# Two Q products moved behind the first half of the attention, and the gate/up pieces of the second half re-ordered

## The chip, the cores and the metric

One Trainium2 chip, one core of it. The metric is the device time of one execution in microseconds (us). The kernel before takes 743.94 us (median of 3 runs, 742.64 to 744.77). The sets of rounds ran on different chips, so each kernel is compared with the kernel before in its own rounds.

## The reference, cut to what matters

```python
x = A_x                                     # 1 x 2048 x 1024, bfloat16
def _A_ref(x, wqkv, wo):                    # linear attention, 32 heads of 32
    q, k, v = ...                           # x @ wqkv
    pq, pk = phi(q), phi(k)                 # phi(t) = where(t > 0, t + 1, exp(t)) + 1e-6
    kv = einsum("bhsd,bhse->bhde", pk, v);  z = einsum("bhsd->bhd", pk)
    o = (pq . kv) / (pq . z + 1e-6)
    return o.reshape(B, S, D) @ wo
def _B_ref(x, W_gate, W_up, W_down):        # inner size 3584
    return (relu(x @ W_gate) * (x @ W_up)) @ W_down
h  = x + _A_ref(_layernorm(x), A_wqkv, A_wo)
h2 = h + _B_ref(_layernorm(h), B_W_gate, B_W_up, B_W_down)
```

All tokens go through kv and z first; then each token needs Q, the denominators and numerators ("nd"), the output projection with wo, a layer norm, and the gate/up and down products.

## The kernel before

It computes the large products with a Strassen-like scheme of seven block products instead of eight. `strassen` is a generator: each `yield` ends a "piece" (mostly eight matmuls of 128x512), and the caller chooses what stands between two pieces. `A`, `E`, `D` are PSUM banks, `snap` is a copy of a bank by ScalarE, `fin` ends one quarter of the result.

```python
def strassen(pool, work, mm, fin, sbufs=3):
    ...
    for v in range(2):
        A[v] = pool.tile(...); mm(A[v], 1, v, True); snap(v, "m1")
    yield
    m2(0)
    for v in range(2):
        mm(A[v], 6, v, False); snap(v, "u2")
    m2(1)
    yield
    for v in range(2):
        E[v] = pool.tile(...); mm(E[v], 5, v, True)
    yield
    for v in range(2):
        mm(A[v], 7, v, False); snap(v, "u3"); fin(1, 1, v, E[v], snaps["u3", v])
    yield
    for v in range(2):
        mm(A[v], 4, v, False); fin(1, 0, v, A[v], None)
    yield
    for v in range(2):
        mm(E[v], 3, v, False); fin(0, 1, v, E[v], snaps["u2", v])
    yield
```

The attention works on 16 tiles of 128 tokens, in steps. In step n the five stages below run for tiles n, n-1, n-1, n-2 and n-4 (`LAG`):

```python
def nd():        # 8 matmuls of 128x132 in 3 banks "ab"; ScalarE Ln and Exp give 1/den (rd);
                 # VectorE writes o_sb = nd * rd (2 buffers)
def oT():        # DMA transpose of o_sb
def x_in():      # loads x_res (3 buffers)
def wo_h(borrow):# "attn": 2 x 8 matmuls in a bank "ab", or "E" when borrowed (steps 8 to 11);
                 # VectorE adds the residual into x_res; ScalarE normalizes into hn (2 buffers)
def hn_T():      # DMA transpose of hn into hnT; then the left sums hs for gate/up (VectorE)
```

Two Q units (of six pieces) for the second half's tokens are spread over the first eight steps as filler, the first gate/up units ("quads", of six pieces) over the later ones. The first piece of a quad, `begin`, also makes eight weight sums on VectorE.

```python
rest = [p for s in range(1, NS) for c in range(0, KH, 2) for p in [q_unit(s, c)] * 6]   # 12 pieces
for step in range(QSTEPS):                                                             # 8 steps
    now = rest[step * len(rest) // QSTEPS:(step + 1) * len(rest) // QSTEPS]
    ...
    attn_step(step)
    if step:                # eight loads of gate/up weights, 512 KB each
        for _ in range(-(-len(early_loads) // (QSTEPS - step))):
            early_loads.pop(0)(held[step][0:1, 0:1])
    for p in now:
        next(p)
...
for step in range(QSTEPS, ready):            # steps 8 to 11
    if step == QSTEPS:
        flow.pop(0)()                        # begin of the first quad
    attn_step(step)
for n in range(steps):                       # steps 12 to 19, 23 pieces
    attn_step(ready + n)
    for p in flow[n * len(flow) // steps:(n + 1) * len(flow) // steps]:
        p()
```

A scheduler then orders each engine's instructions; the order on TensorE is not just that of the program. In the profiles the Q products are line 438 (454 after the change), nd 511 (527), attn 541 (557), the first quads' products 705 (726), the main gate/up stage 785 (810).

## Time and profile before

| stretch | us | PE busy | what runs |
|---|---|---|---|
| 0 to 150 | 150 | | K, V, Q of the first half |
| 150 to 195 | 45 | 43.6 | attention, first half; Q pieces as filler |
| 195 to 222 | 27 | 23.4 | steps 8 to 11, almost no filler |
| 222 to 291 | 69 | 66.9 | attention, second half; gate/up pieces as filler |
| 291 to 737 | 446 | 444.3 | gate/up and down, TensorE without gaps |

The page of the kernel before: busy us and share of the span of each engine, then the granted TensorE clock in 40 slices.

```profile
PE 721.8 (97%) x3967; PEld 382.0 (52%) x4020; DVE 563.2 (76%) x991; ACT 322.0 (43%) x580; POOL 5.7 (1%) x44
PEclk9999999999999999999999999999999999999999
```

There are 4020 weight loads but 3967 matmuls: 53 matmul records are missing from this trace. They show as holes of one matmul without a releaser and are no idle time.

The windows view of the kernel before (start:end, length, busy us of PE, PEld, DVE, ACT and POOL with their counts, granted clock, DMA share, GB/s), for the three stretches that the change touches:

```profile
150.00:195.00 45.00, 43.60 (x238) 21.14 (x241) 31.13 (x74) 34.36 (x87) 1.58 (x7) 1.00 0.94 199
195.00:222.00 27.00, 23.40 (x132) 11.52 (x134) 24.32 (x71) 21.68 (x70) 0.31 (x1) 1.00 0.84 194
222.00:291.00 69.00, 66.92 (x320) 30.65 (x324) 50.39 (x124) 41.16 (x94) 0.00 (x0) 1.00 0.56 146
```

The waits of TensorE in the kernel before, 150 to 291 us: who waited, for whom, us in total, times, longest.

```profile
PE Eq L705 <- DVE hs L117: 2.0, 1, 2.0
PE Aq L438 <- ACT u L154: 1.1, 1, 1.1
PE nd L511 <- DVE o_sb L518: 1.0, 2, 0.8
PE Aq L705 <- ACT m L154: 0.7, 1, 0.7
PE Aq L705 <- ACT u L154: 0.6, 2, 0.3
PE attn L541 <- DVE o_sb L518: 0.4, 1, 0.4
PE attn L541 <- DMA oT<-o_sb: 0.3, 1, 0.3
```

The first two lines are what the change aims at. The timeline of TensorE in the kernel before shows both places (start, length, instruction, count, idle time before it and its releaser):

```profile
186.28 1.46 PE L438 MATMUL Aq<-xT,tq 128*128 128x512 bf16 x5 [1.10 <-ACT u L154]
...
216.79 0.51 PE L511 MATMUL nd<-kvz,pq_mem 128*128 128x132 bf16 x6
218.06 0.28 PE L511 MATMUL nd<-kvz,pq_mem 128*128 128x132 bf16 x2 [0.76 <-DVE o_sb L518]
220.34 0.59 PE L705 MATMUL Eq<-hs,tg 128*128 128x512 f16 x2 [2.00 <-DVE hs L117]
```

What ends the second wait stands in the chain of waits of the kernel before, 204 to 224 us (start, length, what):

```profile
212.57 1.24 ACT hn L557
...
215.62 4.21 DMA hn<-hn
...
219.85 0.44 DVE hs L117
...
220.34 0.59 PE Eq L705 x2
```

The last normalized tile of the first half is made, transposed by DMA, summed on VectorE, and only then can gate/up product 5 start.

**How lost time is counted here.** The timeline merges matmuls, and the modelled length of one (379 ns) is longer than the distance of two starts (216 ns), so short gaps hide in it. All sums of lost time below add, over single matmuls, the start-to-start distance beyond N/2.4 GHz + 2.5 ns, where that is over 60 ns, without one-matmul holes. That cadence is what the Trainium skill gives in "TensorE: Matmul & The Clock Gate", section "Wait — 56ns, not 53.3ns?"; traces agree (eight matmuls in 1.73 us).

### The profile page before, as it was taken

Reading aid. Unit: us, or ns where it says so; the run is one execution under the profiler, and the core shown is the slowest. Engines: PE = TensorE matmul, PEld = TensorE weight load, DVE = VectorE, ACT = ScalarE, POOL = GpSimd, SP = SyncE. Lnnn points to the kernel's source line nnn. Section 1 sums busy time; section 2 is a strip of 40 time slices with the busy share of each in tenths; the row PEclk is TensorE's granted clock in tenths of the full one; section 3 lists DMA queues with packets and bytes.
Section 4 is the critical chain, followed back from the end, with each engine's and each line's share of the span. In section 5 each row is a group of like instructions: output and inputs, shape, how many; then the busy total and the mean of one; then the engine's idle time right before and its main releaser. Section 6 shows DMA issues by size and latency. Waiting matters only on the chain.

```text
span 740.6 us, 10570 instructions
## 1 busy us (share of the span) xinstructions
PE 721.8 (97%) x3967; PEld 382.0 (52%) x4020; DVE 563.2 (76%) x991; ACT 322.0 (43%) x580; POOL 5.7 (1%) x44
## 2 busy tenths in 40 slices
PE   7999999999989999999999999999999999999997
PEld 3444555444444444444444444444444458888666
DVE  6997653675887767778778777877787479996797
ACT  4786553778686654444344434443435120000000
POOL 0000000000000000000000000000000000000000
PEclk9999999999999999999999999999999999999999
DMA  9765003079797526164638359475483399988822
GB/s 319 167 140 157 0 1 107 9 155 242 152 223 165 138 73 203 46 181 137 196 127 233 109 181 288 162 221 201 170 271 127 124 396 345 326 286 298 300 79 79
DMA packets 146579, 132.03 MB, mean 178 GB/s; under 512 B 50912, under 2 KB 128096, under 8 KB 146528
## 3 DMA queue, kind: packets, MB, share of 16 engines
q1 hardware_dynamic: 135392, 123.23, 55.3%
q10 hardware_dynamic: 11136, 8.13, 3.4%
q8 instruction: 31, 0.51, 0.3%
q14 instruction: 20, 0.16, 0.1%
HBM read 79.95 MB, written 39.85 MB: 162 GB/s over the span
## 4 chain that ended last, share of the span: by engine, by line
PE 78%; DVE 8%; ACT 7%; DMA 5%; issue 2%; SPq 0%; DVEq 0%; POOL 0%; ACTq 0%
PE accA L785 22%; PE accX L785 8%; PE accY L785 8%; PE accA L1117 8%; PE Aq L298 3%; PE accA L946 3%; PE accX L1117 3%; PE Aq L438 3%; DMA hn<-hn 2%; PE accY L1117 2%; PE attn L541 2%; PE Aq L705 2%; PE Eq L298 2%; PE accY L946 2%; PE accX L946 2%
## 5 line engine op out<-in xcount | busy, mean ns | idle before, releaser
L795 ACT ACTIVATE gu<-gu 128x512 bf16<-128x512 bf16 x72 | 45.4, 631 | 131.5 <-DVE gu L794 131.5
L790 ACT COPY snap<-accA 128x1024 f32<-128x1024 f32 x72 | 72.5, 1008 | 36.3 <-PE accA L785 36.2
L785 PEld LDWEIGHTS <-tg 128*128 128x128 f16 x384 | 37.6, 98 | 45.3
L785 PEld LDWEIGHTS <-tu 128*128 128x128 f16 x384 | 37.6, 98 | 45.3
L541 PE MATMUL attn<-wo_mem,oT 128*128 128x512 bf16 x249 | 57.9, 379 | 1.2 <-DVE o_sb L518 0.4
L794 DVE TENSOR_TENSOR gu<-accY,snap 128x1024 bf16<-128x1024 f32 x36 | 43.9, 1219 | 10.0 <-ACT snap L790 10.0
L785 PE MATMUL accA<-hn,tu 128*128 128x512 f16 (+1 forms) x192 | 49.3, 379 | 0.0
L785 PE MATMUL accA<-hn,tg 128*128 128x512 f16 (+1 forms) x192 | 49.3, 379 | 0.0
L794 DVE TENSOR_TENSOR gu<-accX,snap 128x1024 bf16<-128x1024 f32 x36 | 43.9, 1219 | 6.2 <-PE accX L785 3.7
L154 ACT COPY u<-Aq 128x512 f32<-128x512 f32 x56 | 32.4, 582 | 37.3 <-PE Aq L298 19.3
L1117 PEld LDWEIGHTS <-x 128*128 128x128 f16 (+1 forms) x448 | 43.8, 98 | 5.5
L785 PEld LDWEIGHTS <-wg 128*128 128x128 bf16 x288 | 28.2, 98 | 34.0
L785 PEld LDWEIGHTS <-wu 128*128 128x128 bf16 x288 | 28.2, 98 | 34.0
L541 PEld LDWEIGHTS <-oT 128*128 128x128 bf16 x256 | 24.6, 98 | 30.8 <-issue 2.9
L798 DVE TENSOR_TENSOR hq<-gu 128x512 bf16<-128x512 bf16 x48 | 20.3, 423 | 14.3 <-ACT gu L795 14.2
L298 PEld LDWEIGHTS <-xT 128*128 128x128 bf16 (+1 forms) x192 | 18.6, 98 | 23.7 <-issue 2.3
L1117 PEld LDWEIGHTS <-xs 128*128 128x128 f16 x280 | 27.4, 98 | 3.2
L543 DVE SCALAR_TENSOR_TENSOR x_res<-attn,x_res 128x512 bf16<-128x512 f32 x32 | 21.8, 687 | 7.2 <-PE attn L541 7.1
L946 PEld LDWEIGHTS <-x 128*128 128x128 bf16 (+1 forms) x168 | 16.4, 98 | 19.6
L518 DVE TENSOR_TENSOR o_sb<-nd,rd 128x384 bf16<-128x384 f32 (+1 forms) x48 | 22.8, 507 | 4.5 <-ACT rd L517 4.4
L1123 DVE TENSOR_TENSOR snap<-accA,u 128x1024 f32<-128x1024 f32 x16 | 19.5, 1220 | 8.3 <-PE accA L1117 8.0
L785 PE MATMUL accA<-hn,wu 128*128 128x512 bf16 x96 | 24.6, 379 | 0.0
(232 smaller groups left out, 1400.8 us busy)
## 6 DMA issues: line engine op xcount, KB each, us to landing
x<-x_dram SPq DMA_DIRECT2D x17, 896.0 KB, 8.2
x_dram<-hq SPq DMA_DIRECT2D x28, 512.0 KB, 3.1
wg<-in_B_W_gate_dram SPq DMA_DIRECT2D x14, 512.0 KB, 5.2
wu<-in_B_W_up_dram SPq DMA_DIRECT2D x14, 512.0 KB, 7.3
wraw<-in_B_W_down_dram SPq DMA_DIRECT2D x14, 512.0 KB, 4.8
x_dram<-hq SPq DMA_DIRECT2D x28, 256.0 KB, 2.6
t_dram<-wt SPq DMA_DIRECT2D x28, 256.0 KB, 2.2
xd<-x_dram SPq DMA_DIRECT2D x6, 896.0 KB, 7.1
```

The lines of the kernel that those rows point to most:

```text
L154: nc.scalar.copy(out=snaps[nm, v], in_=A[v][:])
L298: nc.tensor.matmul(ps[:], lhsT=left[m - 1][:, kc, r + v * P:r + (v + 1) * P], rhs=right[m - 1][:, kc, :], start=(start and kc == 0), stop= ...
L438: nc.tensor.matmul(ps[:], lhsT=rq[m - 1][:, kc, (c + v) * P:(c + v + 1) * P], rhs=left[m - 1][:, kc, :], start=(start and kc == 0), stop=( ...
L518: nc.vector.tensor_tensor(out=ov[:, c0:c0 + n], in0=ndv[:, :, 0:P].rearrange("p k (h e) -> p k h e", h=HPC), in1=rd[:, 0:n, :].unsqueeze(3 ...
L541: nc.tensor.matmul(ps[:], lhsT=st["oT"][:, c, :], rhs=wo_sb[:, c, j * NW:(j + 1) * NW], start=(c == 0), stop=(c == KC - 1))
L543: nc.vector.scalar_tensor_tensor(out=h_sb[:, j * NW:(j + 1) * NW], in0=ps[:], scalar=1.0, in1=h_sb[:, j * NW:(j + 1) * NW], op0=ALU.mult, ...
L785: nc.tensor.matmul(ps[:, v, :], lhsT=w[v][n - 1][:, kc, :], rhs=left[n - 1][:, kc, :], start=(t is not None and kc == 0), stop=(kc == KH - ...
L790: nc.scalar.copy(out=st[nm][:], in_=halves(st["A"]))
L794: add(out=g[:], in0=halves(st[nm]), in1=st[base][:], op=ALU.add)
L795: nc.scalar.activation(out=g[:, 0, :], in_=g[:, 0, :], func=ACT.Relu)
L946: nc.tensor.matmul(ps[:, t * NW:(t + 1) * NW], lhsT=x_tile(n, s, kh)[:, f, (t0 + t) * P:(t0 + t + 1) * P], rhs=w_tile(n, kh)[:, f, :], sta ...
L1117: nc.tensor.matmul(pv[:, tt, :], lhsT=left(m)[:, f, tt * P:(tt + 1) * P], rhs=right(m)[:, f, :], start=(t is not None and f == 0 and tt % ...
```

## The change

Products 7 and 4 of the last Q unit feed only tokens that are needed from step 12 on. They are postponed to steps 8 and 9, where TensorE had little to do. For that, product 3 goes ahead of them, and ScalarE copies the bank after product 5 instead of after product 7, so product 4 no longer waits for a copy. The first quad begins two steps later. From step 12 on each step has three gate/up pieces, with the output projection between the first and the second, and the transpose of hn stands ahead of the rest of the step.

```diff
+        if late:                       # in strassen, after product 5 (and its snap "e5")
+            for v in range(2):
+                mm(E[v], 3, v, False)
+                fin(0, 1, v, E[v], snaps["u2", v])
+            yield
+            for v in range(2):
+                mm(A[v], 7, v, False)
+                fin(1, 1, v, A[v], snaps["e5", v])
+            yield
+            for v in range(2):
+                mm(A[v], 4, v, False)
+                fin(1, 0, v, A[v], None)
+            yield
+            return
 ...
+    last = rest[-2:]
+    del rest[-2:]
 ...
+    for step in range(QSTEPS, QSTEPS + 2):
+        attn_step(step)
+        next(last.pop(0))
 ...
-    for step in range(QSTEPS, ready):
-        if step == QSTEPS:
+    for step in range(QSTEPS + 2, ready):
+        if step == QSTEPS + 2:
             flow.pop(0)()
         attn_step(step)
     for n in range(steps):
-        attn_step(ready + n)
-        for p in flow[n * len(flow) // steps:(n + 1) * len(flow) // steps]:
-            p()
+        attn_step(ready + n, (4, 0, 1, 2))
+        if n:
+            flow.pop(0)()
+        attn_step(ready + n, (3,))
+        for _ in range(2):
+            flow.pop(0)()
```

More of the change, by code (lines that the diff above doesn't have):

```diff
@@ L142, in hold, with strassen, snap @@
         nc.gpsimd.tensor_copy(out=dst, in_=src)
-    def strassen(pool, work, mm, fin, sbufs=3):
+    def strassen(pool, work, mm, fin, sbufs=3, late=False):
         A, E, snaps = {}, {}, {}
-        def snap(v, nm):
+        def snap(v, nm, bank=A):
             if v == 0:
@@ L153, in snap @@
             with tc.high_priority():
-                nc.scalar.copy(out=snaps[nm, v], in_=A[v][:])
+                nc.scalar.copy(out=snaps[nm, v], in_=bank[v][:])
         def m2(v):
@@ L174, in strassen @@
             mm(E[v], 5, v, True)
+            if late:
+                snap(v, "e5", E)
         yield
+        if late:
+            for v in range(2):
[11 more added lines that the diff above has]
+            return
         for v in range(2):
@@ L447, in fin @@
                 phi_end(pair, e[:])
-        return strassen(pspool, qw[-1], mm, fin)
+        return strassen(pspool, qw[-1], mm, fin, 3, s == NS - 1 and c + 2 == KH)
     with tc.tile_pool(name="qwork0", reuse_waits="tile", bufs=2, side="right") as pool:
@@ L568, in block_kernel, with attn_step @@
     begin_at = [n if n < STS else n - STS + QSTEPS for n in range(ST)]
-    def attn_step(step):
-        for k in range(len(LAG)):
+    def attn_step(step, parts=range(len(LAG))):
+        for k in parts:
             n = step - LAG[k]
@@ L743, in block_kernel @@
     for n in range(steps):
-        attn_step(ready + n)
-        for p in flow[n * len(flow) // steps:(n + 1) * len(flow) // steps]:
-            p()
+        attn_step(ready + n, (4, 0, 1, 2))
[4 more added lines that the diff above has]
+            flow.pop(0)()
+    assert not flow
     pqctx.close()
```

## The prediction

> **What bounds the kernel now.** TensorE: the page gives PE 721.8 us busy of a 740.6 us span (97%), granted clock 1.0. From 291 us on the chain of waits is PE alone: what an earlier stage saves is kept whole. A 128x512 matmul starts every 216 ns (8 in 1.73 us in the chain), as the Trainium skill, "TensorE: Matmul & The Clock Gate", section "Wait — 56ns, not 53.3ns?", states for a warm array; the change keeps all matmuls. Only PE gaps can be won. I took start-to-start distances over that cadence from the timeline, without holes of just one matmul and no releaser (lost records). From 150 to 291 us, the stretch touched, PE loses 9.6 us.
>
> **Where those are.**
> 1. 150 to 195 us (first-half attention, Q products as filler): 2.2 us, of which 1.27 at 184.8: Q product 4 accumulates on the bank that product 7 has just filled and waits for ScalarE's copy of it.
> 2. 195 to 222 us (four attention steps almost without filler): 4.6 us. The last first-half projection ends near 208.3; its residual, normalization on ScalarE (3.3 us), transpose (issued 215.6, landed 219.8) and left sums end at 221.4: 13.1 us, while the PE order has 9.2 us of work between it and gate/up product 5. The waits view shows 2.0 us for hs, 1.0 for o_sb.
> 3. 222 to 291 us: 2.8 us, waits of 0.4 to 0.9 us for snapshots on ScalarE and for o_sb.
>
> **What the change does.** It adds and removes no matmul. The last Q unit copies product 5 instead of 1+6+7 (again two copies of 0.58 us). Products 7 and 4 (1.73 us each) feed tokens needed only from step 12 and go to steps 8 and 9. The changed instruction order shows 12.6 us of PE work between the last first-half projection and product 5 (9.2 before), and a whole projection (3.45 us) between products 7 and 4. In the second half projections stand between pieces (often behind 7, ahead of 4), so that snapshots are made under them; hn transposes are issued ahead of the x loads.
>
> **Costed.** Part 1: the 1.27 us go; the first eight steps have 3.5 us less filler while ScalarE is 8.7 of 10 us busy and DMA saturated (share 1.0), so about 0.5 us of new waits: -0.8. Part 2: 13.1 us of latency against 12.6 of work leaves 0.5; VectorE runs the left sums behind the residual of the tenth projection, another 0.5; 4.6 becomes 1.5: -3.1. Part 3: 2.8 becomes 1.6: -1.2. Sum about -5 us, all on the critical path.
>
> **Prediction:** 739.0 us, 8 in 10 between 736.5 and 742.0. Faster by over 2% (under 729.1) can't come from 9.6 us of gaps: 0.01; within 2% 0.98; slower 0.01.
>
> **What would show it.** The main stage's start (first accA matmul, 291.3 before) moves to about 286.3, all behind it by the same; PE busy stays near 721. The wait of Q's Aq for ACT u (1.1 us) is gone; Eq's for hs falls from 2.0 to under 1. For part 3, waits of Aq for ACT m/u after 222 us fall from 1.3 to under 0.7 us.
>
> **What would make it wrong.** Transposes under the weight loads (issue up to 3.2 us) could be late for projections that come 2 to 5 us earlier. The phi work of the postponed products (about 3.6 us of VectorE) could delay o_sb in steps 8 to 11, where VectorE is over 9 of 10 us busy. Gate/up sums write memory freed by the Q weights and must wait for product 4. Each could eat 1 to 3 us; together the whole gain.

## The result, and the profile after

740.70 us (median of 4 runs, 739.40 to 741.56) against 743.38 us for the kernel before in 4 runs; ratio 0.996, 95% interval 0.9936 to 0.9985: within 2%, and faster by some 3 us. A second set of six runs of the same kernel gave 740.44 against 743.92 us, ratio 0.9954. Ratios are the mean time of one kernel's runs over that of the other's of the same rounds, so not quite the ratio of the medians quoted.

The page after has the same work on TensorE:

```profile
PE 721.6 (98%) x3967; PEld 381.8 (52%) x4020; DVE 563.5 (76%) x991; ACT 323.4 (44%) x580; POOL 5.6 (1%) x44
```

The windows view after, same stretches and columns: PE gains 1.9 us of busy time in the middle one, and almost nothing in the others.

```profile
150.00:195.00 45.00, 43.81 (x240) 20.99 (x242) 31.47 (x74) 34.11 (x93) 1.77 (x8) 1.00 0.95 209
195.00:222.00 27.00, 25.33 (x142) 12.38 (x143) 25.35 (x71) 23.65 (x67) 0.00 (x0) 1.00 0.85 190
222.00:291.00 69.00, 67.23 (x322) 31.01 (x327) 50.86 (x125) 42.16 (x93) 0.00 (x0) 1.00 0.55 143
```

The waits of TensorE after, 150 to 291 us:

```profile
PE attn L557 <- DVE o_sb L534: 1.3, 4, 0.6
PE attn L557 <- DVE x_res L559: 0.7, 1, 0.7
PE Aq L726 <- ACT m L154: 0.7, 1, 0.7
PE nd L527 <- DVE o_sb L534: 0.5, 1, 0.5
PE Eq L726 <- DVE hs L117: 0.3, 1, 0.3
PE Aq L726 <- DVE hh L740: 0.2, 1, 0.2
```

The two targets went from 2.0 to 0.3 us and from 1.1 us to nothing. In their place projections wait for o_sb (0.4 us before, 1.3 now) and for the residual x_res (new, 0.7). The timeline of TensorE after shows the new wait in step 10 to 11 and the shrunken one:

```profile
207.75 3.61 PE L557 MATMUL attn<-wo_mem,oT 128*128 128x512 bf16 x15
212.10 0.59 PE L557 MATMUL attn<-wo_mem,oT 128*128 128x512 bf16 x2 [0.74 <-DVE x_res L559]
213.18 0.34 PE L527 MATMUL nd<-kvz,pq_mem 128*128 128x132 bf16 x3 [0.48 <-DVE o_sb L534]
...
218.52 0.59 PE L726 MATMUL Eq<-hs,tg 128*128 128x512 f16 x2 [0.30 <-DVE hs L117]
```

What VectorE did meanwhile, in its timeline after: the residual of the last first-half projection, the first and the last of the eight weight sums of `begin`, two more instructions, and only then the residual that frees the next projection's bank. The eight matmuls that fill this bank were done by about 209.7 (started at 207.75, 216 ns apart).

```profile
206.27 0.68 DVE L559 SCALAR_TENSOR_TENSOR x_res<-attn,x_res 128x512 bf16<-128x512 f32 x1
...
208.01 0.42 DVE L635 TENSOR_TENSOR tg<-wg 128x512 f16<-128x512 bf16 x1
...
210.35 0.42 DVE L641 TENSOR_TENSOR tu<-wu,tu 128x512 f16<-128x512 bf16 x1
210.69 0.42 DVE L117 TENSOR_TENSOR hs<-hn 128x512 f16<-128x512 bf16 x1
211.02 0.42 DVE L217 TENSOR_SCALAR e<-e 128x1024 bf16<-128x1024 bf16 x1
211.36 0.69 DVE L559 SCALAR_TENSOR_TENSOR x_res<-attn,x_res 128x512 bf16<-128x512 f32 x1
```

The first line matters too. The last projection of the first half has its last matmul behind it at 203.75 us, and the chain to its left sums starts with this residual, 2.5 us later. In the kernel before the two stand at 207.56 and 208.48, 0.9 us apart.

Lost time of TensorE from the first nd matmul (146 us) to the main stage, counted as said above (us), one trace each:

| kernel | to 195 | 195 to 222 | 222 to main stage | sum | half rate | first nd to main stage |
|---|---|---|---|---|---|---|
| before | 2.20 | 4.43 | 2.80 | 9.43 | 0 | 144.87 |
| after | 2.25 | 2.15 | 2.19 | 6.60 | 0 | 141.94 |
| after, again ("both") | 2.13 | 2.98 | 2.16 | 7.27 | 0 | 142.60 |
| postpone_only | 2.30 | 2.14 | 2.50 | 6.93 | 0 | 142.22 |
| interleave_only | 1.64 | 4.90 | 2.86 | 9.40 | 1.48 | 146.25 |
| one_late | 5.05 | 4.66 | 3.09 | 12.80 | 1.48 | 149.68 |
| zero_late | 2.34 | 3.86 | 4.96 | 11.16 | 0 | 146.46 |
| loads_later | 2.09 | 3.42 | 2.43 | 7.94 | 0 | 143.26 |
| one_late_loads_later | 3.07 | 4.82 | 3.60 | 11.49 | 1.05 | 147.86 |
| sums_after_projection | 2.08 | 2.72 | 2.17 | 6.98 | 0 | 142.31 |
| projection_first | 6.96 | 2.28 | 3.23 | 12.47 | 1.2, of which 0.9 is in the sum | 148.20 |
| third_o_sb | 5.74 | 2.70 | 2.15 | 10.59 | 0 | 145.99 |
| before_warm | 1.78 | 3.48 | 3.70 | 8.96 | 0 | 145.82 |
| before_repeats | 2.21 | 4.45 | 2.62 | 9.28 | 0 | 146.04 |

The column "half rate" holds the excess of matmuls that were slow from end to end; in interleave_only, one_late and one_late_loads_later those slowed in part add 0.2, 0.2 and 0.5 us, which are in the sums.

Before to after: +0.05, -2.3 and -0.6 us, together -2.8. In the unchanged kernel's second trace the middle stretch is 0.8 us worse: so much does one trace differ from another.

### The profile page after: what moved, and what is told of

Read it like the earlier page. It is cut to its first block, busy times and chain, and to the rows that moved or that the text cites. A ratio compares the mean times of both kernels' runs of the same rounds, so it can differ in the third digit from the quotient of the medians. Undisturbed runs are those within 1.5% of the kernel's fastest.

```text
span 738.1 us, 10551 instructions
## 1 busy us (share of the span) xinstructions
PE 721.6 (98%) x3967; PEld 381.8 (52%) x4020; DVE 563.5 (76%) x991; ACT 323.4 (44%) x580; POOL 5.6 (1%) x44
## 4 chain that ended last, share of the span: by engine, by line
PE 78%; DVE 9%; ACT 6%; DMA 5%; issue 1%; SPq 0%; another core or an unknown queue 0%; DVEq 0%; POOL 0%; ACTq 0%
PE accA L810 22%; PE accY L810 8%; PE accX L810 8%; PE accA L1142 8%; PE attn L557 4%; PE Aq L314 3%; PE accA L971 3%; PE accX L1142 3%; PE Aq L454 3%; PE accY L1142 2%; PE Eq L314 2%; DMA hn<-hn 2%; PE accY L971 2%; PE accX L971 2%; DVE x_res L559 1%
## 5 line engine op out<-in xcount | busy, mean ns | idle before, releaser
L810 PE MATMUL accA<-hs,tu 128*128 128x512 f16 x96 | 24.6, 379 | 0.0
```

Source lines behind the costliest of these rows:

```text
L810: nc.tensor.matmul(ps[:, v, :], lhsT=w[v][n - 1][:, kc, :], rhs=left[n - 1][:, kc, :], start=(t is not None and kc == 0), stop=(kc == KH - ...
```

## The experiments

Theory A: what pays is the work that stands on TensorE between the last projection of the first half and the first product that needs its left sums, since a chain of 13 us (residual, normalization, transpose, sums) has to be hidden under it. From the instruction orders that work is 9.2 us before and 12.6 us after. (`zero_late`, below, has 10.9.) Rivals are named with each experiment. Times are medians.

| run | us | before, same rounds | ratio (95%) |
|---|---|---|---|
| both | 740.44 | 743.92 | 0.9954 (0.9937 to 0.9971) |
| postpone_only | 741.03 | 743.92 | 0.9963 (0.9945 to 0.9981) |
| interleave_only | 744.16 | 743.92 | 1.0002 (0.9985 to 1.0020) |
| one_late | 747.15 | 743.92 | 1.0047 (1.0027 to 1.0067) |
| loads_later | 740.96 | 744.28 | 0.9959 (0.9945 to 0.9973) |
| one_late_loads_later | 745.49 | 744.28 | 1.0024 (1.0010 to 1.0039) |
| before_warm | 744.59 | 744.28 | 1.0005 (0.9990 to 1.0020) |
| sums_after_projection | 739.80 | 744.28 | 0.9941 (0.9929 to 0.9954) |
| zero_late | 745.73 | 744.07 | 1.0025 (1.0009 to 1.0041) |
| projection_first | 745.96 | 744.07 | 1.0034 (1.0019 to 1.0050) |
| third_o_sb | 745.06 | 744.07 | 1.0017 (1.0002 to 1.0032) |
| before_repeats | 744.99 | 744.38 | 1.0007 (0.9990 to 1.0024) |

### 1. The two halves of the change

**both**: the changed kernel, no edit.

> The changed kernel once more, as the yardstick of its own rounds. Both theories: about 2.9 us under the kernel before (four runs gave 740.7 against 743.4).

**postpone_only**, against the changed kernel:

```diff
-        attn_step(ready + n, (4, 0, 1, 2))
-        if n:
-            flow.pop(0)()
-        attn_step(ready + n, (3,))
-        for _ in range(2):
-            flow.pop(0)()
+        attn_step(ready + n)
+        for p in flow[n * len(flow) // steps:(n + 1) * len(flow) // steps]:
+            p()
```

> Products 7 and 4 postponed and product 5 copied, second half as before. Theory A (the postponement brings most: between the first denominators product and the first gate/up product 5 the two traces differ by 2.3 us, the rest by 0.7): 2.0 to 2.5 us under before, 0.5 to 0.9 over the whole change. Rival B (the new order of the second half brings most, and what the first half gains is only shifted into waits of the second): under 1 us of gain. Interaction would show if this and the other half do not add up to the whole within 0.7 us.

**interleave_only**, against the kernel before: the same lines the other way round and the argument `parts` of `attn_step` that they need, nothing else.

> Only the second half's order changed (three pieces per step, projection between first and second, hn transposed first), Q unit as before. Theory A: 0.4 to 1.0 us under before (2.8 us of TensorE gaps from 222 us on become about 2.1). Rival B: 2 us or more. Waits on snapshots (Aq for ACT m or u) after 222 us fall from 1.3 to about 0.7 us.

Measured: 740.44, 741.03 and 744.16 us; before 743.92. The postponement alone brings 2.9 us by medians, the whole change 3.5, the new order of the second half alone nothing (+0.2). That is Theory A's picture and not rival B's, though 2.9 us is more than the 2.0 to 2.5 expected. The two halves add up to 2.7 us, 0.8 less than the whole; 0.7 was to count as a sign that they work on each other, but with intervals of about 1.3 us to either side this stays open. The lower bound expected of interleave_only, 0.4 us, was missed: from 222 us on its lost time is 2.86 us, against 2.80 before. The waits for snapshots did fall, from 1.3 to 0.7 us, as expected, but a wait of 0.8 us of Dq for VectorE's gu came in their place.

Its trace shows something else, which the trace of the kernel before had not. TensorE's timeline in interleave_only, and the windows view of the same place (granted clock is the column before the last two):

```profile
218.43 0.28 PE L511 MATMUL nd<-kvz,pq_mem 128*128 128x132 bf16 x2 [1.00 <-DVE o_sb L518]
220.13 0.73 PE L705 MATMUL Eq<-hs,tg 128*128 128x512 f16 x2 [1.42 <-DVE hs L117]
220.66 1.91 PE L705 MATMUL Aq<-hs,tg 128*128 128x512 f16 x4
```

```profile
216.60:220.20 3.60, 1.04 (x10) 0.65 (x9) 3.54 (x12) 3.47 (x11) 0.00 (x0) 1.00 0.90 235
220.20:223.80 3.60, 3.60 (x10) 1.30 (x10) 3.54 (x10) 2.73 (x9) 0.00 (x0) 0.53 0.99 230
```

After 3.6 us in which TensorE was busy for just 1.0 us, some eight matmuls start 427 ns apart instead of 216, and the granted clock is 0.53. That costs 1.5 us here (1.7 with two matmuls that were slowed in part) and reads as fully busy in the PE column. The idle stretch is the one that the postponement shrinks, so the rate became a question of its own (part 3). But idling alone does not decide it. The windows view of the kernel before, same place, shows just as idle a stretch and no half rate behind it:

```profile
216.60:220.20 3.60, 0.98 (x10) 0.62 (x9) 2.97 (x11) 3.36 (x12) 0.00 (x0) 1.00 1.00 264
220.20:223.80 3.60, 3.46 (x16) 1.55 (x16) 3.60 (x11) 3.26 (x7) 0.00 (x0) 1.00 1.19 212
```

What else must come together is not shown by these runs.

### 2. How much is postponed

**one_late** and **zero_late**, against the changed kernel (only the lines that differ; in both, `begin` moves up accordingly):

```diff
-    last = rest[-2:]
-    del rest[-2:]
+    last = rest[-1:]                 # one_late; in zero_late `last` and its loop are gone
+    del rest[-1:]
-    for step in range(QSTEPS, QSTEPS + 2):
+    for step in range(QSTEPS, QSTEPS + 1):
```

> Only product 4 is postponed (to step 8), product 7 stays in the first eight steps; the rest as in the changed kernel. If the gain comes from filler in the attention steps 8 and 9, proportional to what is moved: about 1 us slower than the whole change, with more PE idle before gate/up product 5. If the filler taken out of the first eight steps costs as much there as it brings later (the new waits of projections for o_sb, 1.4 us in the trace): equal to the whole change within 0.5 us or faster.

> The changed kernel with nothing postponed: the last Q unit's new product order (3 before 7 before 4, product 5 copied) and the second half's new order stay, but all twelve pieces are in the first eight steps. Its TensorE order has about 9 to 11 us of work between the last first-half projection and the first product that needs the left sums, as the kernel before has (9.2; the changed kernel 12.6). Theory A (that distance is what pays): no gain, 743 to 746 us, with 2 us or more of wait for hs. Rival G (not having to wait for the copy of 1+6+7 pays): 741.5 to 743.

Measured: 747.15 and 745.73 us, both slower than the kernel before. zero_late's time fits Theory A, and rival G falls: without the wait for the copy of product 7 it still loses 2.34 us up to 195 us (2.20 before), 0.7 of them to a new wait for ScalarE's e. But its waits are not for hs, as Theory A had it: it loses 3.1 us to waits of projections for oT and 2.8 us to waits for o_sb, mostly from 200 us on. The first lines of its waits view, 150 to 291 us:

```profile
PE attn L557 <- DMA oT<-o_sb: 3.1, 3, 2.0
PE attn L557 <- DVE o_sb L534: 2.8, 3, 2.3
```

one_late fits neither of its two expectations (about +1 us or equal); it is 6.7 us above the whole change. Its TensorE order has the same 9.2 us of work behind the last first-half projection as the kernel before, and its wait for hs is 2.9 us, followed by half-rate matmuls (1.5 us). So far Theory A. Most of the rest is one wait of 2.8 us at 192 us, for a transpose. The chain of waits of one_late, and its queue of DMA issues at that place (length is that of the issue):

```profile
188.85 6.24 DMA oT<-o_sb
195.13 4.50 PE attn L557 x20
```

```profile
188.16 0.57 SPq L502 DMA_DIRECT2D wu<-in_B_W_up_dram  x1
188.85 3.34 SPq L541 DMA_TRANSPOSE oT<-o_sb  x1
...
195.58 1.23 SPq L541 DMA_TRANSPOSE oT<-o_sb  x1
```

Here the transpose issued right behind a 512 KB weight load took 3.34 us to issue, the next one 1.23. In the traces of all kernels, 146 to 291 us, 39 transposes stand within 0.25 us behind such a load in the queue and took 1.6 to 4.0 us to issue (median 2.9); 354 followed something else and took 1.2 to 2.4 (median 1.2).

**loads_later** (against the changed kernel) and **one_late_loads_later** (the same edit on one_late): the four loads of the second gate/up group, not needed before step 16, move to steps 12 and 13.

```diff
-        if step:
-            for _ in range(-(-len(early_loads) // (QSTEPS - step))):
-                early_loads.pop(0)(held[step][0:1, 0:1])
+        if 1 <= step <= 4:
+            early_loads.pop(0)(held[step][0:1, 0:1])
 ...
         attn_step(ready + n, (4, 0, 1, 2))
+        if n < 2:
+            for _ in range(2):
+                early_loads.pop(0)(held[ready + n][0:1, 0:1])
```

> The changed kernel, the four weight loads of the second gate/up group moved from steps 4 to 7 to steps 12 and 13; TensorE's order is the same. Theory C (transposes of the attention are slow while weights load, and late o_sb and oT make the new waits of 1.4 us in the first eight steps): these waits fall by half, 0.7 to 1 us faster than the changed kernel. Rival D (the waits come from the three PSUM banks that denominators and projections share, loads or not): within 0.3 us of the changed kernel.

> The variant with only product 4 postponed (747.2 us), with the same loads moved. In its trace a transpose issued just behind a weight load took 3.3 us to issue and 6.2 us to land, and TensorE waited 2.8 us for it; later came 3.0 us for hs and a stretch of matmuls at half rate. Theory C: at least 3 us of its loss come back (744 or less). Rival D: it stays at 746 to 748, its loss is one of order.

Measured: loads_later 740.96 us, as good as the changed kernel; the lost time up to 195 us is 2.09 us with, 2.13 to 2.25 us without the loads there, and each single wait for o_sb is still in place. (From 195 to 222 us it loses more, 3.42 us, 1.0 of them in a new wait for ScalarE's pq_mem.) Theory C falls for the small waits of the changed kernel. Up to 195 us two of its transposes do stand directly behind loads and took 3.1 and 2.5 us to issue (155.8 and 178.4 us), but no wait of TensorE for a transpose follows that is longer than 0.3 us. one_late_loads_later came down by about 1.7 us (ratio 1.0024 against 1.0047 in other rounds), which is between what Theory C (3 us or more) and rival D (nothing) expected: the wait for oT fell from 2.98 to 0.98 us of lost time, the wait for hs (2.6 us) and the half-rate stretch stayed. So the traces show the transpose behind the load as a part of one_late's loss (by the run times, in different rounds, the 1.7 us are at the edge of the noise); the wait for hs and what follows it is left.

### 3. The rate of the array

Each run lists its granted clock. The 42 runs of the kernel before in the four sets of rounds fall apart by it: 11 at 1.0 with a mean of 742.59 us (741.89 to 743.33), 25 at 0.998 with 744.31 us (743.69 to 744.90), 6 at 0.992 to 0.995 with 745.4 to 747.1 us. The profile that the prediction was read from is one of the first kind. The changed kernel has, in its ten runs with a listed clock, 5 at 1.0 (mean 740.25 us), 3 at 0.999 (739.3 to 741.2) and 2 at 0.998 (741.5). A stretch of 0.53 for 3.6 us, as seen above, is 0.002 of the mean clock.

**before_warm**, against the kernel before (in `early_quad`'s `mm`; the results stay right, since product 5 clears its bank):

```diff
+            if fc == 0 and m == 5 and v == 0:
+                for _ in range(8):
+                    nc.tensor.matmul(ps[:], lhsT=w[0][0][:, 0, :], rhs=left[0][:, 0, :], start=True, stop=True,
+                                     skip_group_check=True)
```

> The kernel before, with eight matmuls of no use (1.73 us) put in front of the first gate/up product 5, into the bank that this product clears, where TensorE idles 2 us for hs. Theory E (in most runs of the kernel before the array drops to half rate for some 3.4 us after this idle stretch, which costs 1.6 to 1.9 us: its runs at granted clock 1.0 take 741.9 to 743.3, those at 0.998 743.9 to 744.9): all runs show clock 1.0 (0.999 or more), and the median falls by 1 to 1.5 us to about 742.7, although work was added. Rival F (the low clock only reports longer waits): the median stays or rises by up to 0.5 us, and clocks of 0.998 and less remain.

**before_repeats**, against the kernel before (in `nd`):

```diff
-                for c in range(c0, c0 + n):
+                for c in [c for c in range(c0, c0 + n) for _ in range(14 if t == order[12] and n == 2 else 1)]:
```

> A gentler repeat of the warm test: the kernel before, with the two last denominator matmuls of the thirteenth tile repeated to 28 (26 more of 58 ns, 1.5 us, same values) just ahead of the gate/up product 5 that idles 2 us for hs. The order of the second half shifts a little again, so only a gain beyond that counts. Theory E: granted clock 0.999 or more in all or nearly all runs (before: 11 of 31 at 1.0), median about 742.7 like the unthrottled runs of the kernel before, 1 us or more under its median. Rival F: clocks of 0.998 stay, or they go and the median does not fall.

Measured: 744.59 and 744.99 us. The clock did what Theory E says: 4 of 5 and 6 of 6 runs are at 0.999 or 1.0, where the kernel before has 11 of 42. (The fifth run of before_warm, at 0.997 and 746.1 us, is the profiled one; its trace has no half-rate stretch between the first nd and the main stage, and its first nd comes 1.8 us late, so its low clock lies before the stretch in question.) The time did not: both medians stay at that of the kernel before. In the traces the added matmuls did not replace idle time. In before_repeats 9.28 us are still lost (9.43 before) and 1.5 us of work came on top; in before_warm 3.70 us are lost from 222 us on, where the order had shifted. So with TensorE kept busy in front of gate/up product 5 the rate stayed up in 10 of 11 runs. But by the terms set beforehand Theory E missed on the time in both runs, and before_repeats came out as rival F had it (the low clocks go and the median does not fall); that the added work ate the gain is an explanation given afterwards. That a low rate costs about 1.7 us is seen in the groups of runs and in four traces (interleave_only, one_late, one_late_loads_later, projection_first: one stretch each of 3.4 us at half the clock, in which matmuls took 1.2 to 1.7 us longer), but no experiment took away the low rate alone and got that time back.

### 4. The waits that are left

**sums_after_projection**, against the changed kernel:

```diff
+        attn_step(step)
         if step == QSTEPS + 2:
             flow.pop(0)()
-        attn_step(step)
```

> The changed kernel, in step 10 the attention stands before the first gate/up piece with its eight weight sums. In the changed kernel VectorE makes these sums (2.7 us) ahead of the ninth projection's first residual, and TensorE waits 0.9 to 1.6 us for the bank that this residual frees. If that order is the cause: this wait goes, 0.5 to 1.2 us faster, unless the first gate/up product 1, now later, leaves TensorE idle while nd and oT come; then it is equal or slower by up to 1 us.

Measured: 739.80 us, ratio 0.9941, the best of all, but its interval overlaps that of the changed kernel (0.9937 to 0.9971) and they ran in different rounds: a gain of about 0.6 us by medians is not shown. Nor does its trace show one: it loses 6.98 us, between the 6.60 and 7.27 us of the changed kernel's two traces. The wait for x_res is gone, as expected; its waits view has, in its place, more waiting of nd for o_sb (0.5 us after the change):

```profile
PE attn L557 <- DVE o_sb L534: 1.3, 4, 0.5
PE nd L527 <- DVE o_sb L534: 1.1, 2, 0.8
PE Aq L726 <- ACT m L154: 0.7, 1, 0.7
PE Eq L726 <- DVE hs L117: 0.4, 1, 0.4
```

**projection_first**, against the changed kernel (first eight steps):

```diff
-        attn_step(step)
+        attn_step(step, (3, 0, 1, 2, 4))
```

> The changed kernel, in the first eight steps the projection of two steps ago is put ahead of the denominators of the step, so that in the ring of three PSUM banks that both take from it waits for o_sb of the step before instead of the same step. Theory D (the new waits of projections for o_sb in the first eight steps, 1.4 to 1.5 us, come from that ring): they go, 0.7 to 1.4 us faster. Rival H (VectorE and ScalarE are simply late with o_sb, whatever the ring): the waits move to the denominators, equal within 0.4 us.

**third_o_sb**, against the changed kernel (memory for one more buffer was free only for a while, so tiles 2 and 5 use it):

```diff
+    qo = q1ctx.enter_context(tc.tile_pool(name="qo", reuse_waits="tile", bufs=1, side="right"))
-            o_sb = bwork.tile([P, D], BF16, tag="o_sb", name="o_sb")
+            o_sb = (qo if order.index(t) in (2, 5) else bwork).tile([P, D], BF16, tag="o_sb", name="o_sb")
```

> The changed kernel with a third buffer for o_sb in the first eight steps. In its trace the third step's o_sb starts at 156.40, right after the transpose that reads the first step's o_sb landed at 156.28, and the first projection, which needs the PSUM bank that this o_sb frees, starts at 157.0 after 0.7 us of idling. If the o_sb buffers are behind it: this one wait (0.7 us) goes, the later ones of 0.1 to 0.4 us stay or halve, 0.4 to 1.0 us faster. If PSUM banks alone: unchanged within 0.4 us.

Measured: 745.96 and 745.06 us, both over 4 us worse than the changed kernel. None of the expectations held in size. One wait is settled: in both kernels the first projection, which had lost 0.71 us waiting for o_sb, now loses 0.71 and 0.68 us waiting for oT itself, so neither the banks (Theory D) nor the o_sb buffers were its cause. The later small waits are not settled: third_o_sb gives a third buffer to two tiles only, and the order on TensorE changed in both kernels. The waits view of third_o_sb, first lines:

```profile
PE attn L558 <- DMA oT<-o_sb: 4.1, 3, 3.4
PE attn L558 <- DVE o_sb L535: 1.1, 3, 0.5
```

Our reading, argued from that first wait: PSUM banks and o_sb buffers only show where the projection is held; what is too long for the filler between is the chain behind them: nd, two ScalarE steps, o_sb, transpose. Rival H of projection_first had the waits move to the denominators: that is its largest one, 3.6 us of nd for x_res (and then 3.4 us at half the clock). Both kernels still have the 12.6 us of work in the middle; what they lose, they lose mainly up to that one long wait each brings, which ends at 194 and 198 us. In third_o_sb it is again a transpose right behind a weight load (issue 3.10 us, 6.04 us from issue to landing); in projection_first such a transpose (issue 3.37 us) stands there too, but whether the wait for x_res follows from it was not tried.

## Why the prediction was right or wrong

The range (736.5 to 742.0 us) held both medians, 740.7 and 740.4. The direction, the place and the main mechanism were right; the gain was called 5 us and was 2.7 to 3.5 us by medians, 2.8 us by lost time in the traces (2.2 in the second trace). That the median still fell into the range owes much to its width: gains of 1.9 to 7.4 us lay in it. And about 1.3 us of the gain by run times came with the clock (last point but one), which the prediction did not cost; that part is luck.

- **The bound.** Right. TensorE's work is unchanged, the main stage starts 2.5 us earlier (first accA at 291.1 before, 288.6 after; called: 286.3), and the last matmul ends 2.5 us earlier (736.7 and 734.2). Nothing is given back later.
- **Part 2, called -3.1 us, measured -2.3 (and -1.5 in the second trace).** The mechanism is right: the wait for hs fell from 2.0 to 0.3 us, and zero_late and one_late, with 10.9 and 9.2 us of work there instead of 12.6, lose all of the gain (each of them to other waits as well). The step that failed is "13.1 us of latency against 12.6 of work": the latency grew. From the end of the last first-half projection to product 5 the traces have 12.8 us before, 14.8 after and 15.5 in the second trace; less the work, that leaves the time lost in between (3.6, 2.2 and 2.9 us). It grew mostly at its head. The residual of that projection starts 0.9 us after it before, and 2.5 and 3.2 us after it now: VectorE first waited for a transpose of hn (1.0 and 1.8 us) and then had sums, phi and o_sb ahead of it. The next projection's wait for its bank (0.9 and 1.6 us, behind eight weight sums of 2.7 us) is a place where this lost time shows, and hardly an extra: in sums_after_projection it is gone, and the distance is still 15.3 us. The prediction named the phi work as a danger, but for o_sb, and these sums only as readers of freed memory.
- **Part 1, called -0.8 us, measured 0.** The 1.27 us for the copy did go. The step that failed is "about 0.5 us of new waits": the shorter filler made 1.3 us of them (o_sb, four to five places of 0.1 to 0.7 us). They are not the weight loads (loads_later). The first and largest is not the three banks (projection_first) nor the two buffers (third_o_sb), but the chain up to oT with too little work in front of it; for the others that is argued, not shown.
- **Part 3, called -1.2 us, measured -0.6, and nothing when done alone.** Snapshot waits after 222 us fell from 1.3 only to 0.7 us instead of below, and projections lose 0.36 and 0.54 us there waiting for o_sb, where before one lost 0.55. Half of the 0.6 us came with the postponement alone (2.50 us lost in postpone_only). The re-ordering moves waits more than it removes them.
- **Not in the prediction: the rate.** Compared at clock 1.0 the change is worth 742.59 - 740.25 = 2.3 us. Over all runs with a listed clock the means are 744.1 and 740.5 us, 3.6 us apart. The other 1.3 us go with the more frequent low clock of the kernel before. This part is read from groups of runs, not isolated by an experiment.
- **Of the dangers named,** transposes under weight loads are real (one_late, third_o_sb); the changed kernel has two in its first eight steps that were slow to issue, but no long wait came of them.

## What to carry to other kernels

Filler belongs where the longest chain of other engines has to be hidden, and the gain can be estimated as that chain's length less the TensorE work that the instruction order puts over it, if the chain is taken as it is after the change (here 14.8 us, not the 12.8 before it); but the place that the filler is taken from pays, and here it paid about as much as it saved. Look at what stands ahead of the instruction that starts a chain or frees a buffer, not only at how busy its engine is. And look at every run's granted clock before comparing two medians one per cent apart: an idle stretch can cost a second time, in matmuls at half rate that look busy.

## What the Trainium skill lacked or had wrong

- "TensorE: Matmul & The Clock Gate", section "Why this matters for your kernels", asks for no idle gaps over about 3 us between bursts of matmuls. Here half rate came behind two shorter gaps, of 1.00 and 1.42 us with two matmuls of 128x132 between them: TensorE busy 1.04 of 3.6 us, then 3.4 us of matmuls at 427 ns instead of 216. Behind gaps of 0.76 and 2.00 us at the same place in the kernel before, busy 0.98 of 3.6 us, it did not come. So neither the longest gap nor the busy time of such a stretch decided alone.
- No page says how half rate shows in runs without a profile: here the granted clock of a whole run, 0.998 instead of 1.0, goes with 1.7 us (744.31 and 742.59 us, means of 25 and 11 runs).
- "DMA: Bandwidth & Descriptors", section "Rules for kernel authors", says that a transpose next to ordinary DMAs needs nothing. That is about correctness, and all results were right, but no page says what such a neighbour costs in issue time: 39 DMA transposes of 128x1024 directly behind a 512 KB load took 1.6 to 4.0 us to issue (median 2.9), the 354 that followed no such load 1.2 to 2.4; two of the slow ones took 6.0 and 6.2 us to land (median of the oT transposes in the kernel before: 3.4).
